# Sums of k's features on halves of TensorE's columns, numerators on their own, projections side by side in a linear-attention and mixture kernel

## The chip, the cores and the metric

The kernel runs on one core of a Trainium2 chip. The metric is the device time of one execution in microseconds (us), lower is better.

## What is computed

The reference, cut to its three stages (B = 8, H = 8 heads, S = 576 positions, D = 64, 128 features):

```python
def phi(x):
    proj = einsum('bhsd,df->bhsf', x, w_phi)
    proj = proj - max(abs(proj), axis=-1, keepdims=True)
    return concatenate([exp(proj), exp(-proj)], axis=-1)
q_p, k_p = phi(q), phi(k)
kv = einsum('bhsf,bhsd->bhfd', k_p, v)          # sums of k's features, with
z = sum(k_p, axis=2)                            # their denominators
num = einsum('bhsf,bhfd->bhsd', q_p, kv)        # numerators
den = einsum('bhsf,bhf->bhs', q_p, z)[..., None] + 1e-06
x = (num / den), heads put side by side         # (8, 576, 512)
# mixture 1: xk, xr from x and x shifted by one; sigmoid(xr @ w_r) * (relu(xk @ w_k)**2 @ w_v)
# mixture 2: sigmoid(causal convolution of 5 taps) * (x @ w_val), then @ w_out
```

## The kernel before

Everything lies in one function, `build`. It doesn't issue instructions in the order of its text. It adds tasks to an `Order` (L99): each names an engine, an assumed duration, what it reads and writes, the new buffers it takes, and a due time. `run` (L129) then walks through time: for every engine it takes, among the tasks sorted by due time, the one that can start first by the assumed durations, and emits its instructions. So each engine has a fixed order, written out ahead; on the chip the instructions wait for one another by semaphores. The due times stand in the table `T` (L33), counted in pairs: `sums=-0.37` means that the sums of pair j are due at j - 0.37.

**The attention stage** works on 32 pairs of heads, j = 0 to 31. Two pairs (n = j // 2) share one load of q, k and v (`load_t` L394, `load_v` L407). For each pair TensorE does these tasks:

- `q_proj`, `k_proj` (L479, L469), both through `proj` and `project` (L418): eight matmuls that contract over 64 rows. The two heads of a pair lie on partitions 0 to 63 and 64 to 127, so one matmul uses the upper half of the array's rows and the next one the lower half. `tails` (L450) does the last 64 positions of q and k for two pairs at once, eight matmuls every second pair. Each takes two PSUM banks of the tag "pj", of which four may be held (`PSB` L241).
- `q_tails`, `q_turn` (L482, L500): ten transposes that turn q's projections.
- `kv` (L520): the sums. Twenty matmuls, each with a stationary block of 128 positions by 128 features (one of exp and exp of the negative) and 65 moving columns of v (64 and a column of ones). The operands are plain f32, and each such matmul is two weight loads and two matmuls in the trace.
- `num` (L562): the numerators, four groups of six matmuls with 288 moving columns and a stationary block of 65 columns, in f32r (one matmul instruction each).

`kv` is called four times a pair, i = 0 to 3, with five sums each, and hands them to `together` (L587), which alternates them with one group of numerators of the pair before: product, sum, product, sum. After the last sums ScalarE and VectorE split the result into a high and a low part (`kvh`, `kvl`), the stationary blocks of the numerators.

The other engines' part: VectorE takes the maximum and subtracts it (`centre` L426), ScalarE does the exponentials and copies, GpSimd subtracts the high parts (`less_far` L271). From pair 2 to 24 the weights of the mixtures are narrowed and split as well (`convert` L339): ScalarE, four operations on VectorE, GpSimd, two transfers a piece, 28 pieces in all. All transfers in this stage are issued by SyncE (SP).

**The mixture stage** (`moe` L678) works on 16 blocks of 288 positions; its matmuls (`gemm` L663, `st_v` L751) have 288 moving columns.

The line that the change is about:

```python
mm(out=b[:, o:o + 65], lhsT=lhs, rhs=vt[:, a:a + 65], start=(k == 0), stop=(c == 3), skip_group_check=True)
```

Of the kernel before, what the change touches and what calls it, by code (L numbers as in the profile page):

```python
# [18 lines left out]
NP = 2 * NQ  # L19
S = 576  # L20
TB = 288
# [4 lines left out]
def pattern(bits):  # L26
# [3 lines left out]
LEAST, MOST = pattern((896 + 128) << 20), pattern(((1150 + 128) << 20) | 0xFFFFF)  # L30


T = dict(load_q=-2.59, load_k=-2.65, load_v=-1.31, tails=-1.05, q_proj=-1.29, k_proj=-1.16, q_tails=-0.19,  # L33
         q_turn=(-0.15, 0.1), sums=-0.37, finish=1.77, convert=0.24)
FROM, TO = 2, 25

LAST = ("pj", "qp", "kv", "cv")
# [3 lines left out]
DMA_START = 1.3  # L41
DMA_END = 1.0
DMA_RATE = 350e3


class Buf:
# [52 lines left out]
class Order:  # L99
# [3 lines left out]
        self.tasks, self.slots, self.queue, self.banks = [], slots, {}, banks  # L103
        self.last_write, self.reads, self.now = {}, {}, 0.0

    def add(self, eng, dur, fn, r=(), w=(), new=(), at=None, dma=0):
        t = {"eng": eng, "dur": dur, "fn": fn, "deps": set(), "at": self.now if at is None else at,
             "id": len(self.tasks), "new": list(new), "dma": dma, "end": None,
             "bufs": set()}
        for x in r:  # L110
            t["deps"].update(self.last_write.get(x, ()))
        for x in w:
            t["deps"].update(self.reads.pop(x, ()))
            t["deps"].update(self.last_write.get(x, ()))
        for x in r:
            self.reads.setdefault(x, []).append(t["id"])
        for x in w:
            self.last_write[x] = [t["id"]]
        for b in new:
            self.queue.setdefault(b.tag, []).append((b, t["id"]))  # L120
        for x in itertools.chain(r, w):
            b = x[0] if isinstance(x, tuple) else x
            if isinstance(b, Buf):
                b.users.append(t["id"])
                t["bufs"].add(b)
        t["deps"].discard(t["id"])
        self.tasks.append(t)

    def run(self):  # L129
        tasks = self.tasks  # L130
        place = {tag: {b: k for k, (b, _) in enumerate(q)} for tag, q in self.queue.items()}
        taken = dict.fromkeys(self.queue, 0)
        free, dma_free = {}, 0.0
        todo = {}
        for t in tasks:
            todo.setdefault(t["eng"], []).append(t)
        for q in todo.values():
            q.sort(key=lambda t: (t["at"], t["id"]))

        def ready(t):  # L140
            at = 0.0
            for d in t["deps"]:
                d = tasks[d]
                if d["end"] is None:
                    return None
                at = max(at, d["end"] + (SAME if d["eng"] == t["eng"] else SEM))
            if any(b.tile is None and b not in t["new"] for b in t["bufs"]):
                return None
            ahead = {}
            banked = [b for b in t["new"] if b.tag in self.banks.most]  # L150
            if banked:
                t["found"] = self.banks.when(tasks, banked)
                if t["found"] is None:
                    return None
                at = max(at, t["found"][-1][0])
            for b in t["new"]:
                k = place[b.tag][b]
                if k != taken[b.tag] + ahead.get(b.tag, 0):
                    return None
                ahead[b.tag] = ahead.get(b.tag, 0) + 1  # L160
                if b.tag in self.banks.most:
                    continue
                old = k - self.slots[b.tag]
                if old >= 0:
                    for u in self.queue[b.tag][old][0].users:
                        u = tasks[u]
                        if u["end"] is None:
                            return None
                        at = max(at, u["end"] + SEM)
            return at  # L170

        left = len(tasks)
        while left:
            best = None
            for eng, q in todo.items():
                f = free.get(eng, 0.0)
                got = None
                for t in q[:400]:
                    at = ready(t)
                    if at is None:  # L180
                        continue
                    at = max(at, f)
                    if got is None or at < got[0] - 1e-9:
                        got = (at, t)
                        if at <= f:
                            break
                if got and (best is None or got[0] < best[0]):
                    best = got
            at, t = best
            banked = [b for b in t["new"] if b.tag in self.banks.most]  # L190
            if banked:
                t["rel"] = {u for _, _, old in t["found"] if old is not None for u in old.users}
                self.banks.take(t["found"], banked)
            for b in t["new"]:
                taken[b.tag] += 1
                if b.tag not in self.banks.most:
                    b.tile = b.make()
            t["fn"]()
            free[t["eng"]] = at + t["dur"]
            t["end"] = at + t["dur"]  # L200
            if t["dma"]:
                dma_free = max(dma_free, at + DMA_START) + t["dma"] / DMA_RATE
                t["end"] = dma_free + DMA_END
            todo[t["eng"]].remove(t)
            if not todo[t["eng"]]:
                del todo[t["eng"]]
            left -= 1
# [27 lines left out]
def build(ctx, tc, qt, kt, vv, wphi, mu, wk, wr, wv, wval, cw, wout, out):  # L235
# [12 lines left out]
    add = G.add  # L248
# [186 lines left out]
    def proj(x, j, tag):  # L435
        n, p = divmod(j, 2)
        bs = [ps("pj"), ps("pj")]
        if tag == "dq":
            t = sb("kl", [128, 2, 4, 128])
            ds = [(lambda ab=ab: t[:, ab], (t, ab), [] if ab else [t]) for ab in range(2)]  # L440
        else:
            ts = [sb(tag, [128, 4, 128]) for _ in range(2)]
            ds = [(lambda t=t: t[:], t, [t]) for t in ts]
        add("PE", 1.08, lambda: project(bs, x[n], [p * 512 + 128 * i for i in range(4)], 0),
            r=cols_of(x[n], n, p) + [("wph", 0), ("wph", 1)], w=bs, new=bs)
        for ab in range(2):
            centre(bs[ab], ds[ab], 4)
        return [d[:2] for d in ds]

    def tails(j):  # L450
# [5 lines left out]
            for i, x in enumerate((qs, ks)):  # L456
                project(bs, x[n], [1024], i)

        add("PE", 0.64, go, r=cols_of(qs[n], n, 2) + cols_of(ks[n], n, 2) + [("wph", 0), ("wph", 1)], w=bs, new=bs)
        for ab in range(2):  # L460
            centre(bs[ab], (lambda ab=ab: d[:, ab], (d, ab), [] if ab else [d]), 2)
        st[j]["dt"] = d
# [57 lines left out]
    def kv(j, i):  # L520
# [12 lines left out]
        def one(k):  # L533
# [5 lines left out]
            else:  # L539
                a = 1040 + 130 * ab + 65 * p  # L540
                lhs = et[:, ab, half, :]
            mm(out=b[:, o:o + 65], lhsT=lhs, rhs=vt[:, a:a + 65], start=(k == 0), stop=(c == 3), skip_group_check=True)  # L542

        mine = list(range(len(todo) * i // 4, len(todo) * (i + 1) // 4))
        need = {ab for c, ab, _ in (todo[k] for k in mine) if c is not None}
        reads = [(s["ek", x], half) for x in need for half in range(2)]
        if any(todo[k][0] is None for k in mine):
            reads += [(et, 0), (et, 1), (vk, "t", 0), (vk, "t", 1)]
        if need:
            reads += [(vk, 0)]  # L550
        here = [] if i else [("pair", j)]
        together(next(st[j - 1 if i else j - 2]["num"]) if j > (0 if i else 1) else None, [lambda k=k: one(k) for k in mine], reads + [(vk, "ones")], [b, *here],
                 [] if i else [b])
        if i < 3:
            return
        h, l = (sb(t, [128, 260], F32R) for t in ("kvh", "kvl"))

# [26 lines left out]

                yield [lambda i=i, one=one: one(i) for i in range(6)], [*a, *e], b, after

    def together(group, sums, r, w, new):  # L587

        if group is None:
            add("PE", 0.217 * len(sums), lambda: [f() for f in sums], r=r, w=w, new=new)  # L590
            return
        prods, reads, b, after = group

        def go():
            for i in range(max(len(prods), len(sums))):
                for f in prods[i:i + 1] + sums[i:i + 1]:
                    f()

        add("PE", t_mm(TB, 6) + 0.165 * len(sums), go, r=r + reads, w=w + [b], new=new + [b])
        after()  # L600

    def finish(j):
# [270 lines left out]
        load(lambda: cwr, lambda: cw.bitcast(I32).rearrange("p (c t) -> p c t", t=2), 20480, w=["cwr"])  # L873
        narrow(lambda: cwr, lambda: cwt, 20, ("cwr", "cwt"))

    def last_num():
        for i, j in enumerate([NP - 2] + [NP - 1] * 4):
            G.now = NP + T["sums"] + i / 8
            together(next(st[j]["num"]), [], [], [], [])

    for j in range(NP):
        n, p = divmod(j, 2)
        st[j] = {}
# [7 lines left out]
        due(j + T["q_tails"], q_tails, j)  # L891
        for ab in range(2):
            due(j + T["q_turn"][ab], q_turn, j, ab)
        for i in range(4):
            due(j + T["sums"] + i / 4, kv, j, i)
        due(j + T["finish"] + 0.5, finish, j)
        if j % 4 == 3:
            due(j + T["finish"] + (1.5 if j < NP - 1 else 0.6), invert, j // 4)
# [2 lines left out]
        if FROM <= j < TO:  # L901
            w = TO - FROM
            for i in range((j - FROM) * len(pieces) // w, (j - FROM + 1) * len(pieces) // w):
                due(j + T["convert"], convert, *pieces[i], j - 1)
    due(NP + T["sums"], last_num)
    for t, _, fn, args in sorted(events, key=lambda e: e[:2]):
        G.now = t
        fn(*args)
# [54 lines left out]
```

## Time and profile before

| | us |
|---|---|
| median of three runs | 1080.18 |
| lowest, highest | 1072.57, 1080.31 |
| profiled execution, its own time | 1071.74 |
| its span, first to last instruction | 1069.8 |

In the profile, TensorE's matmuls are PE and its weight loads PEld; VectorE is DVE, ScalarE ACT, GpSimd POOL, SyncE SP. Matmuls are pipelined: the duration of one reaches into the next, so what a matmul costs is the distance from its start to the next one's start, not its duration. An operand is written as partitions x elements; "128\*65" behind the names is the stationary block's shape, contracted rows by columns.

### The profile page before, as it was taken

What the parts mean: (1) busy time and instruction counts of PE and PEld (TensorE: products, weight loads), DVE (VectorE), ACT (ScalarE), POOL (GpSimd) and SP (SyncE); (2) the same over time, 40 slices, a digit from 0 to 9 for tenths busy, and PEclk for the clock granted to TensorE, in tenths of its full rate; (3) what the DMA queues carried; (4) which work ended last, traced back from release to release, by engine and by line L of the source; (5) the groups of instructions that cost most, each with busy time, mean ns of one, the idle gap of its engine ahead of it and who ended that gap; (6) DMA issues with size and microseconds to landing.
All of it is one profiled execution on the core that took longest, in us unless ns stands there. A gap on an engine that the chain in (4) does not pass through costs nothing.

```text
span 1069.8 us, 22099 instructions
## 1 busy us (share of the span) xinstructions
PE 1060.4 (99%) x8912; PEld 1037.7 (97%) x8912; DVE 739.5 (69%) x1445; ACT 530.6 (50%) x1042; POOL 319.9 (30%) x438
## 2 busy tenths in 40 slices
PE   8999999999999999999999999999999999999998
PEld 8999999999999999999999999999999999999998
DVE  6889898989766486584765847658476584865735
ACT  5888888888878333242332423324233242332423
POOL 3778787888867311101101011010110101100000
PEclk9999999999999999999999999999999999999999
DMA  7567678778835911201112021120211201100001
GB/s 203 143 190 213 186 232 251 233 236 237 251 70 163 311 25 50 62 17 51 45 29 62 15 54 45 29 62 12 56 45 29 61 13 56 45 6 18 13 12 45
DMA packets 88918, 103.71 MB, mean 97 GB/s; under 512 B 44240, under 2 KB 69200, under 8 KB 88432
## 3 DMA queue, kind: packets, MB, share of 16 engines
q1 hardware_dynamic: 88224, 101.64, 32.4%
q8 instruction: 70, 1.15, 0.5%
q10 hardware_dynamic: 592, 0.66, 0.2%
q14 instruction: 32, 0.26, 0.1%
HBM read 72.62 MB, written 29.66 MB: 96 GB/s over the span
## 4 chain that ended last, share of the span: by engine, by line
PE 95%; DMA 3%; DVE 1%; issue 0%; POOL 0%; SPq 0%; ACT 0%; POOLq 0%; ACTq 0%
PE b L673 15%; PE b L672 15%; PE b L671 15%; PE b L542 10%; PE b L577 9%; PE b L423 7%; PE b L764 6%; PE b L762 6%; PE b L763 6%; PE b L507 3%; DMA eh<-wvhl 1%; DMA qf<-xs 1%; DMA el<-wvalhl 1%; PE b L491 1%; PE b L375 0%
## 5 line engine op out<-in xcount | busy, mean ns | idle before, releaser
L282 POOL TENSOR_TENSOR el<-qe,eh 128x288 fp32r<-128x288 f32 x256 | 199.0, 810 | 77.6 <-ACT eh L266 73.2
L717 POOL TENSOR_TENSOR qf<-qf,rb 128x288 f32<-128x288 f32 (+1 forms) x64 | 56.0, 905 | 530.1 <-DMA qf<-xs 445.3
L542 PE MATMUL b<-v,ek 128*128 128x65 f32 x1024 | 158.1, 247 | 0.0
L542 PEld LDWEIGHTS b<-v,ek 128*128 128x128 f32 x1024 | 156.6, 190 | 0.1
L672 PE MATMUL b<-ql,wkh 128*128 128x288 f32 x512 | 151.9, 297 | 0.0
L673 PE MATMUL b<-qh,wkl 128*128 128x288 f32 x512 | 151.8, 296 | 0.0
L671 PE MATMUL b<-qh,wkh 128*128 128x288 f32 x512 | 151.6, 296 | 0.0
L746 ACT ACTIVATE d<-b 128x288 f32<-128x288 f32 x128 | 52.4, 409 | 161.2 <-PE b L673 160.7
L800 DVE SCALAR_TENSOR_TENSOR qh<-kf,cwt,qh 128x288 f32<-128x288 f32 x256 | 124.8, 516 | 2.1
L429 DVE TENSOR_REDUCE m<-b 128x4 f32<-128x512 f32 (+1 forms) x160 | 95.2, 632 | 33.1 <-PE b L423 32.1
L673 PEld LDWEIGHTS b<-qh,wkl 128*128 128x128 f32 x512 | 96.6, 189 | 0.0
L672 PEld LDWEIGHTS b<-ql,wkh 128*128 128x128 f32 x512 | 96.4, 188 | 0.2 <-DVE ql L269 0.2
L671 PEld LDWEIGHTS b<-qh,wkh 128*128 128x128 f32 x512 | 96.3, 188 | 0.0
L511 ACT ACTIVATE qe<-b 128x512 f32<-128x512 f32 x128 | 70.6, 589 | 32.9 <-PE b L507 32.9
L577 PE MATMUL b<-eh,kvh 128*65 128x288 f32 x256 | 86.1, 336 | 0.0
L747 DVE TENSOR_TENSOR d<-d 128x288 f32<-128x288 f32 x64 | 33.4, 522 | 76.1 <-ACT d L746 76.1
L577 PE MATMUL b<-eh,kvl 128*65 128x288 f32 x256 | 83.4, 326 | 0.1
L577 PE MATMUL b<-el,kvh 128*65 128x288 f32 x256 | 83.3, 325 | 0.0
L475 ACT ACTIVATE ek<-d 128x512 f32<-128x512 f32 x128 | 72.9, 620 | 5.7 <-DVE d L431 5.5
L672 PE MATMUL b<-kl,qe 128*128 128x288 f32 x256 | 75.7, 296 | 0.0
L671 PE MATMUL b<-kh,qe 128*128 128x288 f32 x256 | 75.6, 295 | 0.0
L672 PE MATMUL b<-qe,el 128*128 128x288 f32 x256 | 75.4, 295 | 0.0
(146 smaller groups left out, 3056.7 us busy)
## 6 DMA issues: line engine op xcount, KB each, us to landing
xs<-X SPq DMA_DIRECT2D x32, 288.0 KB
kh<-in_kt SPq DMA_DIRECT2D x15, 576.0 KB
qh<-in_qt SPq DMA_DIRECT2D x15, 576.0 KB
v<-in_vv SPq DMA_DIRECT2D x16, 512.0 KB
rb<-rs SPq DMA_DIRECT2D x16, 289.0 KB
qf<-xs SPq DMA_DIRECT2D x8, 578.0 KB
rb<-rs SPq DMA_DIRECT2D x16, 288.0 KB
qf<-xs SPq DMA_DIRECT2D x8, 576.0 KB
```

Of the source, the lines that this page charges most:

```text
L282: nc.gpsimd.tensor_tensor(out=out[:, c], in0=x[:, c], in1=hi[:, c], op=ALU.subtract)
L423: mm(out=bs[ab][:, (at + i) * 128:(at + i + 1) * 128], lhsT=x[r, c:c + 128], rhs=wph[r], start=True, stop=True)
L429: add("DVE", t_dve(128 * n), lambda: nc.vector.tensor_reduce(out=m[:, 0:n, 0], in_=b3[:, 0:n], axis=AX.X, op=ALU.max, apply_absolute_value ...
L475: add("ACT", t_act(512), lambda d=d, e=e, half=half: act(out=e[:, :, half], in_=d(), func=AF.Exp, scale=-1.0 if half else 1.0), r=[tok], w ...
L511: add("ACT", t_act(512), lambda half=half: act(out=e[:, ab, half, 0:512], in_=b[:], func=AF.Exp, scale=-1.0 if half else 1.0), r=[b], w=[( ...
L542: mm(out=b[:, o:o + 65], lhsT=lhs, rhs=vt[:, a:a + 65], start=(k == 0), stop=(c == 3), skip_group_check=True)
L577: mm(out=b[0:65, 0:TB], lhsT=a[x][:, o:o + 65], rhs=e[y][:, half, ts], start=(i == 0), stop=(i == 5))
L671: mm(out=o[:, 0:TB], lhsT=wh, rhs=mov[0][:, c, :], start=(c == 0), stop=False)
L672: mm(out=o[:, 0:TB], lhsT=wh, rhs=mov[1][:, c, :], start=False, stop=False)
L673: mm(out=o[:, 0:TB], lhsT=wl, rhs=mov[0][:, c, :], start=False, stop=(c == kc - 1))
L762: mm(out=o, lhsT=wh, rhs=h(), start=(c == 0), stop=False)
L800: stt(out=g[:, c], in0=a, scalar=cv[:, c, t:t + 1], in1=g[:, c], op0=ALU.mult, op1=ALU.add)
```

## The change

- Every sum is done in two halves of 64 stationary columns: features 0 to 63 go to PSUM partitions 0 to 63, features 64 to 127 to partitions 64 to 127. Each half has the same 65 moving columns. So a sum is four weight loads and four matmuls, with half the columns.
- `together` is gone. The sums come in two tasks a pair, i = 0 (the four tails and the eight sums of the first head) and i = 1 (the eight sums of the second); the numerators are four tasks of six matmuls (`num_step`), due at j + 0.68 and every quarter pair after.
- Tasks carry a mark "split": "rows" for projections, "columns" for sums. When TensorE's last task had a mark, `run` prefers a task with the same mark that can start within 0.6 us and is due within 0.8 pairs of the first in the queue. Entering a split is assumed to take 0.29 us.
- The due times in `T` are others, also those of loads, conversions and stores.

The diff, without the plain change of the constants `SPLIT`, `KV`, `SOON`, `EARLY` to the file's head and without the two lines of `add` that store the mark:

```diff
-T = dict(load_q=-2.59, load_k=-2.65, load_v=-1.31, tails=-1.05, q_proj=-1.29, k_proj=-1.16, q_tails=-0.19,
-         q_turn=(-0.15, 0.1), sums=-0.37, finish=1.77, convert=0.24)
+T = dict(load_q=-2.16, load_k=-2.75, load_v=-1.7, tails=-0.96, q_proj=-1.74, k_proj=-0.93, q_tails=-0.43,
+         q_turn=(-0.11, -0.21), sums=-0.36, num=0.68, finish=1.99, convert=1.07)
...
+SPLIT = 0.29
+KV = 0.125
+SOON, EARLY = 0.6, 0.8
...
+                    if eng == "PE" and split and t["split"] == split and at <= f + SOON and t["at"] <= q[0]["at"] + EARLY:
+                        got = (at, t)
+                        break
                     if got is None or at < got[0] - 1e-9:
                         got = (at, t)
-                        if at <= f:
+                        if at <= f and not (eng == "PE" and split):
                             break
...
+            if t["eng"] == "PE":
+                if t["split"] and t["split"] != split:
+                    t["dur"] += SPLIT
+                split = t["split"]
...
-        add("PE", 1.08, lambda: project(bs, x[n], [p * 512 + 128 * i for i in range(4)], 0),
-            r=cols_of(x[n], n, p) + [("wph", 0), ("wph", 1)], w=bs, new=bs)
+        add("PE", 0.9, lambda: project(bs, x[n], [p * 512 + 128 * i for i in range(4)], 0),
+            r=cols_of(x[n], n, p) + [("wph", 0), ("wph", 1)], w=bs, new=bs, split="rows")
...
-            mm(out=b[:, o:o + 65], lhsT=lhs, rhs=vt[:, a:a + 65], start=(k == 0), stop=(c == 3), skip_group_check=True)
-
-        mine = list(range(len(todo) * i // 4, len(todo) * (i + 1) // 4))
...
+            for y in (slice(0, 64), slice(64, 128)):
+                mm(out=b[y, o:o + 65], lhsT=lhs[:, y], rhs=vt[:, a:a + 65], start=(k == 0), stop=(c == 3),
+                   skip_group_check=True)
+
+        mine = [k for k, (c, ab, _) in enumerate(todo) if (c is None and i == 0) or (c is not None and ab == i)]
...
-        together(next(st[j - 1 if i else j - 2]["num"]) if j > (0 if i else 1) else None, [lambda k=k: one(k) for k in mine], reads + [(vk, "ones")], [b, *here],
-                 [] if i else [b])
-        if i < 3:
+        add("PE", KV * len(mine), lambda: [one(k) for k in mine], r=reads, w=[b, *here], new=[] if i else [b],
+            split="columns")
+        if i < 1:
             return
...
+    def num_step(j):
+        prods, reads, b, after = next(st[j]["num"])
+        add("PE", t_mm(TB, 6), lambda: [f() for f in prods], r=reads, w=[b], new=[b])
         after()
...
+        for i in range(2):
+            due(j + T["sums"] + i / 4, kv, j, i)
         for i in range(4):
-            due(j + T["sums"] + i / 4, kv, j, i)
+            due(j + T["num"] + i / 4, num_step, j)
...
-    due(NP + T["sums"], last_num)
```

## Rows read from the trace of the kernel before

**Rows 1.** The page, part 1: busy time, share of the span, instructions of each engine.

```profile
PE 1060.4 (99%) x8912; PEld 1037.7 (97%) x8912; DVE 739.5 (69%) x1445; ACT 530.6 (50%) x1042; POOL 319.9 (30%) x438
```

**Rows 2.** The page, part 4: the chain that ended last, shares by engine.

```profile
PE 95%; DMA 3%; DVE 1%; issue 0%; POOL 0%; SPq 0%; ACT 0%; POOLq 0%; ACTq 0%
```

**Rows 3.** Windows: length, busy (instructions) of PE, PEld, DVE, ACT, POOL; clock, DMA share, GB/s.

```profile
108.10:245.90 137.80, 137.80 (x1436) 128.75 (x1434) 123.79 (x225) 117.10 (x238) 110.93 (x154) 1.00 0.76 229
288.20:330.50 42.30, 42.30 (x442) 39.53 (x441) 26.67 (x50) 33.55 (x68) 29.00 (x41) 1.00 0.41 96
560.00:760.00 200.00, 200.00 (x1507) 200.00 (x1507) 128.87 (x263) 69.10 (x132) 17.90 (x20) 1.00 0.15 44
```

**Rows 4.** Timeline of PE, projections of k: start us, length us, instructions merged.

```profile
308.27 1.16 PE L423 MATMUL b<-wph,kh 64*128 64x128 f32 x16
...
318.44 1.16 PE L423 MATMUL b<-wph,kh 64*128 64x128 f32 x16
...
329.41 1.16 PE L423 MATMUL b<-wph,kh 64*128 64x128 f32 x16
```

**Rows 5.** Waits from 108.1 to 245.9: us in total, times, longest.

```profile
DVE m L429 <- PE b L423: 6.2, 12, 0.6
DVE X L582 <- PE b L577: 5.0, 8, 0.7
...
ACT qe L511 <- PE b L507: 13.6, 13, 1.2
```

**Rows 6.** Groups of PE by shape, 108.1 to 245.9: busy us, mean ns, idle before.

```profile
L542 PE MATMUL b<-v,ek 128*128 128x65 f32 x416 | 64.6, 246 | 0.0
...
L542 PE MATMUL b<-v,et 128*128 128x65 f32 x104 | 16.2, 247 | 0.0
```

**Rows 7.** Timeline of PE, products and sums in turn.

```profile
304.92 0.33 PE L577 MATMUL b<-el,kvh 128*65 128x288 f32 x1
305.08 0.33 PE L542 MATMUL b<-v,ek 128*128 128x65 f32 x2
...
305.83 0.33 PE L577 MATMUL b<-el,kvh 128*65 128x288 f32 x1
```

**Rows 8.** Timeline of PE, the last 24 products, first and what follows them.

```profile
346.93 0.29 PE L577 MATMUL b<-eh,kvh 128*65 128x288 f32 x1
...
350.10 0.30 PE L671 MATMUL b<-qh,wkh 128*128 128x288 f32 x1
```

**Rows 9.** Timeline of all engines, sums alone at the start.

```profile
20.15 1.06 PE L542 MATMUL b<-v,et 128*128 128x65 f32 x8
...
20.99 1.42 PEld L542 LDWEIGHTS b<-v,ek 128*128 128x128 f32 x12
21.05 1.50 PE L542 MATMUL b<-v,ek 128*128 128x65 f32 x12
```

**Rows 10.** Timeline of PE, projections next to one another at the start.

```profile
7.99 0.39 PE L423 MATMUL b<-wph,qh 64*128 64x128 f32 x4
...
8.44 1.06 PE L423 MATMUL b<-wph,qh 64*128 64x128 f32 x16
```

**Rows 11.** Timeline of PEld, weight loads of products and sums.

```profile
304.89 0.14 PEld L577 LDWEIGHTS b<-el,kvh 128*65 128x65 f32 x1
304.95 0.32 PEld L542 LDWEIGHTS b<-v,ek 128*128 128x128 f32 x2
```

**Rows 12.** Timeline of PE, projections between transposes.

```profile
106.73 0.38 PE L491 MATMUL b<-ident,dq 128*128 128x128 f32 x2
107.04 1.16 PE L423 MATMUL b<-wph,kh 64*128 64x128 f32 x16
108.13 0.66 PE L507 MATMUL b<-ident,kl 128*128 128x128 f32 x4
...
110.36 0.49 PE L423 MATMUL b<-wph,qh 64*128 64x128 f32 x4
...
111.01 0.66 PE L507 MATMUL b<-ident,kl 128*128 128x128 f32 x4
```

More of the change, by code (lines that the diff above doesn't have):

```diff
@@ L104, in __init__, with add @@
         self.last_write, self.reads, self.now = {}, {}, 0.0
-    def add(self, eng, dur, fn, r=(), w=(), new=(), at=None, dma=0):
+    def add(self, eng, dur, fn, r=(), w=(), new=(), at=None, dma=0, split=False):
         t = {"eng": eng, "dur": dur, "fn": fn, "deps": set(), "at": self.now if at is None else at,
-             "id": len(self.tasks), "new": list(new), "dma": dma, "end": None,
+             "id": len(self.tasks), "new": list(new), "dma": dma, "end": None, "split": split,
              "bufs": set()}
@@ L170, in ready @@
             return at
-        left = len(tasks)
+        left, split = len(tasks), False
         while left:
@@ L457, in go @@
                 project(bs, x[n], [1024], i)
-        add("PE", 0.64, go, r=cols_of(qs[n], n, 2) + cols_of(ks[n], n, 2) + [("wph", 0), ("wph", 1)], w=bs, new=bs)
+        add("PE", 0.45, go, r=cols_of(qs[n], n, 2) + cols_of(ks[n], n, 2) + [("wph", 0), ("wph", 1)], w=bs, new=bs, split="rows")
         for ab in range(2):
@@ L541, in one @@
                 lhs = et[:, ab, half, :]
-            mm(out=b[:, o:o + 65], lhsT=lhs, rhs=vt[:, a:a + 65], start=(k == 0), stop=(c == 3), skip_group_check=True)
-        mine = list(range(len(todo) * i // 4, len(todo) * (i + 1) // 4))
-        need = {ab for c, ab, _ in (todo[k] for k in mine) if c is not None}
-        reads = [(s["ek", x], half) for x in need for half in range(2)]
-        if any(todo[k][0] is None for k in mine):
+            for y in (slice(0, 64), slice(64, 128)):
+                mm(out=b[y, o:o + 65], lhsT=lhs[:, y], rhs=vt[:, a:a + 65], start=(k == 0), stop=(c == 3),
+                   skip_group_check=True)
+        mine = [k for k, (c, ab, _) in enumerate(todo) if (c is None and i == 0) or (c is not None and ab == i)]
+        reads = [(s["ek", i], half) for half in range(2)] + [(vk, 0), (vk, "ones")]
+        if i == 0:
             reads += [(et, 0), (et, 1), (vk, "t", 0), (vk, "t", 1)]
-        if need:
-            reads += [(vk, 0)]
         here = [] if i else [("pair", j)]
-        together(next(st[j - 1 if i else j - 2]["num"]) if j > (0 if i else 1) else None, [lambda k=k: one(k) for k in mine], reads + [(vk, "ones")], [b, *here],
-                 [] if i else [b])
-        if i < 3:
+        add("PE", KV * len(mine), lambda: [one(k) for k in mine], r=reads, w=[b, *here], new=[] if i else [b],
+            split="columns")
+        if i < 1:
             return
@@ L585, in num @@
                 yield [lambda i=i, one=one: one(i) for i in range(6)], [*a, *e], b, after
[L587 to L599, printed above, removed]
+    def num_step(j):
+        prods, reads, b, after = next(st[j]["num"])
+        add("PE", t_mm(TB, 6), lambda: [f() for f in prods], r=reads, w=[b], new=[b])
         after()
@@ L874, in small @@
         narrow(lambda: cwr, lambda: cwt, 20, ("cwr", "cwt"))
[L876 to L879, printed above, removed]
     for j in range(NP):
```

## The prediction

> **What bounds the kernel now.** I read the page first. TensorE is busy for 99% of the span [rows 1], and the chain that ended last, followed back, lies on it for 95% of the span [rows 2]. Next the table of windows, because the share is a mean over two stages. In the attention stage with weight conversion (108 to 246 us) TensorE has no idle time, but VectorE is busy 123.79 of 137.80 us and ScalarE 117.10; late in attention (288 to 330 us) VectorE falls to 26.67 of 42.30 us; in the mixture stage (560 to 760 us) TensorE is full again at 200.00 of 200.00 [rows 3]. The granted clock is 1.00 (2.4 GHz) in all of them, so the clock is no term of the sum. The change touches attention alone: I leave the mixture stage, about 345 to 1070 us, as it is.
>
> Attention is a loop over 32 pairs of heads. The timeline of TensorE shows its beat: from one projection of k to the next it is 308.27 to 318.44 us (10.17) and to 329.41 us (10.97); the long one holds the tails [rows 4]. The mean is 10.57 us. The waits of that stage show VectorE and ScalarE waiting for TensorE (6.2, 5.0 and 13.6 us in thirteen pairs) [rows 5]. So the price of TensorE's instructions sets the beat, and VectorE stands close behind it: 123.79 us in thirteen pairs is 9.52 us a pair.
>
> **Sums, before.** A pair has 20 sums, each two weight loads and two matmuls (L542 in the 13 pairs of that window: x416 on ek and x104 on et, so 40 matmuls a pair [rows 6]). They alternate with the numerators' products: three product-and-sum steps take 304.92 to 305.83 us, so 0.303 us a step [rows 7]. Products alone: 24 of them from 346.93 to 350.10 us, 0.132 us each [rows 8]. A sum inside a step therefore costs 0.303 - 0.132 = 0.171 us, and twenty cost 3.42 us. Sums alone go at 0.90 us for 8 matmuls, 0.1125 each, 0.225 a sum [rows 9]. So interleaving gains something today, and the change gives that up.
>
> **Sums, after.** Each sum becomes two halves of 64 columns, one on either half of the array's columns, and the numerators stand by themselves. No row shows columns split. I bound the price from the nearest rows. Below: with the rows split, two instructions run side by side; x8 takes 7.99 to 8.44 us, so 0.1125 us for two matmuls that each move and load 128 columns [rows 10]. Here 65 are moved and 64 loaded, about half: 0.057 a pass, 0.114 a sum of two passes. Above: a load of 65 columns is followed by the next load 0.06 us later (304.89 to 304.95 [rows 11]); if the halves run one after the other, a sum is four such loads, 0.24 us. A gain beyond 0.114 I exclude, since neither loads nor matmuls get shorter than half. I take 0.12, two passes of one 0.06 load, because the split of rows in this very trace shows both halves side by side, and the split of columns is nearest to it. Twenty sums: 2.40 us.
>
> **The price of a split.** One projection of x16 runs 107.04 to 108.13 us, 1.09 us, though 16 matmuls at the side-by-side rate are 0.90; the two transposes before it begin at 106.73 and should take 0.22, but it starts 0.31 later [rows 12]. So entering and leaving costs 0.19 + 0.09 = 0.28 us. The tails, x8 in 110.36 to 111.01 us, are 0.65 instead of 0.45 by the same [rows 12]. For the split of columns I take 0.28 too; below, nothing (gain 0.28 a pair), above, two entries a pair if a pair's two groups stand apart (loss 0.28). I take one, since the second group is due a quarter of a pair behind the first and the order now prefers a task of the same split.
>
> So the sums gain 3.42 - 2.40 - 0.28 = 0.74 us a pair.
>
> **Projections together.** Before, a pair enters the split of rows 2.5 times (q, k, and the tails every second pair, each apart in [rows 4, 12]). After, their due times within a pair are 0.04 (tails), 0.07 (k) and 0.26 (q), close enough to stand together. At startup the trace has such a row of projections: between 7.99 and 8.44 us no entry is paid [rows 10]. But the projections' four PSUM banks hold only two of the three, and VectorE must free one. I take 1.5 entries a pair, a gain of 0.28; the bounds are nothing and 0.42. Whatever TensorE waits to keep them together (the order allows 0.6 us) comes off this.
>
> **What costs nothing, and its cover.** Numerators now follow their own sums by a whole pair, as far as before; kvh and kvl have that pair as cover. Loads of q, k, v, the converted pieces and the stores are only due at other times: the DMA queues are busy 0.76 of the conversion stage [rows 3], so the same bytes in 10% less time are 0.84. Without that cover a late load of q or k (one array of 128 x 1152 words, 0.59 MB) at the stage's 229 GB/s costs 2.6 us every second pair, more than the gain; I see no queue near that. Past SP no more transfers are issued than before.
>
> **The sum.** TensorE needs 0.74 + 0.28 = 1.02 us less, 9.55 us a pair. VectorE needs 9.52 [rows 3], so in conversion (23 pairs, 2 to 24) two engines would be full at once, in fixed orders that wait for each other. I give half of the gain there, 0.51 us: 23 x 0.51 = 11.7. In the other 9 pairs VectorE is at 63% (26.67 of 42.30) and all of it stays: 9 x 1.02 = 9.2. Together 20.9 us. The profiled execution took 1071.74 us (span 1069.8), so 1051 us. The runs' median, 1080.18, lies 0.8% above it, and the fastest, 1072.57, beside it; I stay with the profiled one and let the range reach up.
>
> **Rivals.**
>
> *The halves don't overlap.* Each half's load and matmul take their turn: at 0.24 us a sum (four loads of 0.06; two passes of a 0.06 load and a 0.057 matmul in turn come to 0.234, the same), twenty cost 4.80, the sums lose 1.66 and the projections return 0.28: 1.38 a pair, 44 us in all, 1116 us. The entry (0.28) and the gain of the projections (0.28) cancel, so it turns where twenty sums cost 3.42, at 0.171 us a sum. At 0.20 it is 32 x 0.58 = 19 us, 1090 us. For it: the trace shows only rows split, and 160 short instructions a pair must be issued. Against it: with rows split, eight loads and eight matmuls run in 0.45 us [rows 10]. The Trainium skill's page "TensorE: Matmul & The Clock Gate", Part 3, "The mechanism", says that weight loads overlap running matmuls only when their row groups differ; by that rule two column halves, which share all rows, would load and multiply in turn, and the time would be this rival's. The trace doesn't bear it out for whole-array sums: twelve loads from 20.99 us and twelve matmuls from 21.05 us lie over each other [rows 9]. Chance 0.15.
>
> *VectorE takes over the bound.* In conversion the beat falls only to 10.4 us, because VectorE's own 9.52 us meets PSUM banks that it frees late. 23 x 0.15 + 9 x 0.6 = 9 us, 1063 us, within 1%. For it: the 90% share. Against it: its idle time today ends on TensorE [rows 5], so it has room to follow. Chance 0.21.
>
> *TensorE gains all.* VectorE hides, the tails stand with k and q: 32 x 1.02 = 33 us, 1039 us; a sum at 0.114 (0.12 a pair) and the projections' 0.42 (0.14 more) would add 32 x 0.26 = 8. Chance 0.14.
>
> *The forecast*, a beat of 9.9 to 10.2 in conversion and 9.5 to 9.7 after, 1044 to 1060 us. Chance 0.50.
>
> **How the numbers follow.** About 1% (11 us) is what a measurement of this kernel tells from no change. Faster by more: the forecast (0.50) and all of the gain (0.14), 0.64. Within: VectorE's bound and a mild loss on the halves, 0.22. Slower by more: the rest of the halves' case, 0.14. The range leaves out the two ends: below 1036 those two together, above 1076 most of the first rival. Cases of both signs don't hold most of the chance, but the forecast's own range is 1044 to 1060.
>
> **What would show it.** In the changed profile: 80 matmuls a pair on the sums' line, with loads of 64 columns, whose starts come every 0.03 us on average (right) or 0.06 (rival); one gap of some 0.2 us around them; k, q and tails in one row of projections; a beat near 10.0 in conversion and 9.55 after it, with first idle time of TensorE ahead of projections, ended by VectorE; and a mixture stage of unchanged length. Wrong would be sums longer than 3.4 us a pair, or a beat still at 10.5 with TensorE idle.

## The result, and the profile after

| | kernel before | changed kernel |
|---|---|---|
| median of the runs, us | 1080.08 | 1034.10 |
| lowest, highest | 1072.57, 1080.31 | 1033.65, 1035.54 |
| profiled execution, its own time | 1071.74 | 1034.55 |
| its span | 1069.8 | 1032.7 |

The ratio of the times is 0.959, with an interval of 0.955 to 0.964: 4.1% faster. Beside the runs of the experiments below the kernel before took 1071.35 and 1071.12 us in the median, and the changed kernel 1033.94 and 1035.11: ratios of 0.965 and 0.966, so about 3.5%, the better figure because it rests on more runs. Of those eighteen later runs of the kernel before, the seven with a mean granted clock of 1.000 took 1068.99 to 1070.96 us, the nine at 0.998 took 1070.87 to 1072.22, and the two at 0.992 took 1078.46 and 1078.51. The sign was right; the size was larger than forecast, and 1034.1 us lies just below the range (1036 to 1076). Between the two profiled executions 37.2 us went, where I had worked out 20.9.

The page of the changed kernel, busy time and instructions. Beside [rows 1], TensorE has 1280 more matmuls and weight loads, and is busy for 37 us less:

```profile
PE 1023.4 (99%) x10192; PEld 998.9 (97%) x10192; DVE 731.0 (71%) x1445; ACT 525.5 (51%) x1042; POOL 320.6 (31%) x438
```

The windows of the changed kernel, in the columns of [rows 3]: the middle of conversion, late attention, and 200 us of the mixture stage.

```profile
105.00:230.00 125.00, 124.44 (x1974) 114.85 (x1970) 121.78 (x225) 116.00 (x240) 113.35 (x158) 1.00 0.86 257
...
270.00:310.00 40.00, 39.33 (x602) 36.72 (x601) 28.52 (x51) 36.19 (x74) 31.87 (x42) 1.00 0.54 146
...
520.00:720.00 200.00, 200.00 (x1511) 200.00 (x1510) 130.52 (x267) 69.50 (x133) 17.89 (x20) 1.00 0.15 43
```

The mixture stage runs as before, 1511 matmuls in 200 us against 1507. In conversion VectorE now works for 121.78 of 125 us, and TensorE for 124.44.

The timeline of TensorE in the changed kernel, start and length in us. It answers to [rows 4, 7 and 12]:

```profile
153.31 1.09 PE L519 MATMUL b<-ident,kl 128*128 128x128 f32 x8
...
191.84 1.09 PE L519 MATMUL b<-ident,kl 128*128 128x128 f32 x8
...
197.21 1.16 PE L435 MATMUL b<-wph,qh 64*128 64x128 f32 x16
198.21 1.06 PE L435 MATMUL b<-wph,kh 64*128 64x128 f32 x16
199.20 0.34 PE L588 MATMUL b<-eh,kvh 128*65 128x288 f32 x1
...
200.03 0.38 PE L503 MATMUL b<-ident,dq 128*128 128x128 f32 x2
200.34 0.69 PE L555 MATMUL b<-v,et 128*64 128x65 f32 x16
200.86 2.04 PE L555 MATMUL b<-v,ek 128*64 128x65 f32 x64
202.83 1.09 PE L519 MATMUL b<-ident,kl 128*128 128x128 f32 x8
203.85 1.16 PE L435 MATMUL b<-wph,qh 64*128 64x128 f32 x16
204.94 0.35 PE L588 MATMUL b<-eh,kvh 128*65 128x288 f32 x1
...
208.17 0.38 PE L503 MATMUL b<-ident,dq 128*128 128x128 f32 x2
```

Four pairs now take 153.31 to 191.84 us, 9.63 us a pair; before it was 10.57. A sum is now four matmuls in the trace, two for each half, so a pair has eighty half matmuls. All of them stand in one stretch: 16 need 0.52 us (200.34 to 200.86, the entry of about 0.05 inside), the next 64 need 1.97 with the exit. At 0.117 us a sum (that is 0.0292 for each half matmul, worked out from 64 of them in 1.87 us without the exit of about 0.1) twenty are 2.34; the stretch takes 2.49, and it begins 0.31 us after two transposes that need 0.22. q's and k's projections stand together at 197.21 and 198.21, and q's stands alone at 203.85. The 24 products from 204.94 to 208.17 are 3.23 us.

### The profile page after: what moved, and what is told of

It is laid out like the page before. It is cut to its first block, busy times and chain, and to the rows that moved or that the text cites. A ratio compares the mean times of both kernels' runs of the same rounds, so it can differ in the third digit from the quotient of the medians.

```text
span 1032.7 us, 24612 instructions
## 1 busy us (share of the span) xinstructions
PE 1023.4 (99%) x10192; PEld 998.9 (97%) x10192; DVE 731.0 (71%) x1445; ACT 525.5 (51%) x1042; POOL 320.6 (31%) x438
## 4 chain that ended last, share of the span: by engine, by line
PE 89%; ACT 3%; POOL 3%; DMA 2%; DVE 2%; issue 1%; SPq 0%; POOLq 0%; ACTq 0%
PE b L674 16%; PE b L673 16%; PE b L672 16%; PE b L588 8%; PE b L763 6%; PE b L764 6%; PE b L765 6%; PE b L435 6%; PE b L555 6%; PE b L519 3%; POOL el L294 2%; ACT ek L487 1%; ACT eh L278 1%; DMA qf<-xs 1%; DMA xs<-X 1%
## 5 line engine op out<-in xcount | busy, mean ns | idle before, releaser
L588 PE MATMUL b<-eh,kvh 128*65 128x288 f32 x256 | 77.9, 304 | 0.0
L673 PE MATMUL b<-qe,el 128*128 128x288 f32 x256 | 75.5, 295 | 0.0
L588 PE MATMUL b<-el,kvh 128*65 128x288 f32 x256 | 75.3, 294 | 0.2 <-POOL el L294 0.2
L588 PE MATMUL b<-eh,kvl 128*65 128x288 f32 x256 | 75.2, 294 | 0.0
L672 PE MATMUL b<-qe,el 128*128 128x288 f32 x256 | 75.1, 293 | 0.0
L278 ACT ACTIVATE eh<-qe 128x1152 fp32r<-128x1152 f32 x64 | 74.8, 1168 | 0.0
L673 PE MATMUL b<-eh,X 128*128 128x288 f32 x240 | 70.7, 295 | 0.0
```

The source lines that it names most:

```text
L278: act(out=out, in_=x, func=AF.Copy)
L588: mm(out=b[0:65, 0:TB], lhsT=a[x][:, o:o + 65], rhs=e[y][:, half, ts], start=(i == 0), stop=(i == 5))
L672: mm(out=o[:, 0:TB], lhsT=wh, rhs=mov[0][:, c, :], start=(c == 0), stop=False)
L673: mm(out=o[:, 0:TB], lhsT=wh, rhs=mov[1][:, c, :], start=False, stop=False)
```

## Experiments

Three theories stood against one another after the result. A: TensorE's own instructions set the beat, at 0.117 us a sum and about 0.28 for each entry into a split, and nothing else holds it. B: the order is what gained (numerators apart, projections together, due times), or, in conversion, VectorE takes part of the gain. C: what looks like a price of the split is something else, such as the issue of short instructions. The kernel before ran beside each of three groups. The runs with sums on the full array, with lower halves first and with halves in the old order are one execution each, beside one of the kernel before; the others are medians, beside the changed kernel once more at 1033.94 us (kernel before 1071.35) or 1035.11 us (1071.12).

> The changed kernel once more, as the measure for the three beside it on the same chip: 1033.6 to 1035.6 us, 0.96 of the kernel before.

> The changed kernel once more, as the measure for the three beside it on the same chip: 1033.5 to 1035.5 us.

**Sums on the full array again, in the changed order.**

```diff
-            for y in (slice(0, 64), slice(64, 128)):
-                mm(out=b[y, o:o + 65], lhsT=lhs[:, y], rhs=vt[:, a:a + 65], start=(k == 0), stop=(c == 3),
-                   skip_group_check=True)
+            mm(out=b[:, o:o + 65], lhsT=lhs, rhs=vt[:, a:a + 65], start=(k == 0), stop=(c == 3), skip_group_check=True)
```

> The changed kernel, same order on every engine, but each sum is again one matmul over all 128 columns. Theory A (the halves side by side are the gain): in the kernel before, sums alone cost 0.225 us each [rows 9], in the changed one two halves cost 0.117; 20 x 0.108 = 2.16 us a pair dearer, less about 0.25 for the entry that falls away: 32 x 1.9 = 61 us, 1034 + 61 = about 1095 us, slower than the kernel before. Rival B (the gain is in the order: numerators apart, projections together, other due times): 1035 to 1050 us.

Measured: 1087.38 us, beside 1070.02 for the kernel before. The timeline of TensorE:

```profile
198.43 1.00 PE L554 MATMUL b<-v,et 128*128 128x65 f32 x8
199.27 3.74 PE L554 MATMUL b<-v,ek 128*128 128x65 f32 x32
202.84 1.04 PE L519 MATMUL b<-ident,kl 128*128 128x128 f32 x8
```

The 40 matmuls of a pair take 198.43 to 202.84, 4.41 us, where the 80 halves took 2.49. So theory A holds and B, that the order alone gains, falls: without the halves the new order is 17 us slower than the old one. A sum costs 0.22 us here (4.41 / 20), where it cost 0.171 between products: that the lost cover is the whole reason is argued from these two prices. The time lies 8 us under theory A's number; 0.22 in place of 0.225 a sum is about 3 of them, and the rest is not settled.

**All lower halves first, then all upper ones.**

```diff
-        add("PE", KV * len(mine), lambda: [one(k) for k in mine], r=reads, w=[b, *here], new=[] if i else [b],
+        add("PE", KV * len(mine), lambda: [one(k, y) for y in (slice(0, 64), slice(64, 128)) for k in mine], r=reads, w=[b, *here], new=[] if i else [b],
```

> The changed kernel, but within each task of sums all lower halves come first and then all upper halves. Theory A (two halves overlap only where neighbours in the queue lie on different column halves): each half costs a load or matmul of its own, about 0.058 us where it now shares it, so 0.234 us a sum, 2.34 us a pair, 1034 + 75 = about 1109 us. Rival B (a short load and a short matmul are simply issued at 0.03 us each, whatever half they lie on): 1034 us.

Measured: 1086.49 us. The timeline of TensorE, at a change from lower to upper halves (et is first in each half's row, ek follows) and at the end of a pair's sums:

```profile
210.70 0.92 PE L554 MATMUL b<-v,ek 128*64 128x65 f32 x13
211.41 0.27 PE L554 MATMUL b<-v,et 128*64 128x65 f32 x1
211.46 0.22 PE L554 MATMUL b<-v,ek 128*64 128x65 f32 x1
211.51 0.22 PE L554 MATMUL b<-v,et 128*64 128x65 f32 x1
211.52 0.22 PE L554 MATMUL b<-v,ek 128*64 128x65 f32 x1
211.57 0.22 PE L554 MATMUL b<-v,et 128*64 128x65 f32 x1
211.57 0.22 PE L554 MATMUL b<-v,ek 128*64 128x65 f32 x1
...
213.67 0.86 PE L554 MATMUL b<-v,ek 128*64 128x65 f32 x12
```

Twelve halves on the same columns last 0.86 us, the last one 0.22 of it, so they start every 0.058 us: (0.86 - 0.22) / 11. That is the price theory A gives, 0.234 us a sum, and it rules out theory C, that short instructions are simply cheap to issue. Two things follow. The halves gain only when neighbours in the order lie on different column halves. And 0.058 us is about what one load of 65 columns alone took in the kernel before (0.06 [rows 11]), so load and matmul don't take turns: on the same rows and columns the next load overlaps the running matmul. The total was 23 us under the expectation. Where the order changes from one half to the other, about three matmuls of the second half start among the last of the first, up to 0.16 us early (211.41 against 211.57); I had not thought of that. A pair has three such changes, so that is some 15 of the 23 us; the rest is not settled.

**The halves alone, in the old order.** The kernel before, with the two half matmuls in place of one.

```diff
-            mm(out=b[:, o:o + 65], lhsT=lhs, rhs=vt[:, a:a + 65], start=(k == 0), stop=(c == 3), skip_group_check=True)
+            for y in (slice(0, 64), slice(64, 128)):
+                mm(out=b[y, o:o + 65], lhsT=lhs[:, y], rhs=vt[:, a:a + 65], start=(k == 0), stop=(c == 3),
+                   skip_group_check=True)
```

> The kernel before with the halves alone: sums and numerators still alternate, order as before. Theory A (each change between split and whole array costs about 0.25 us in and out): a step of product and sum costs 0.132 + 0.117 + 0.25 = 0.50 us where it cost 0.303, 20 x 0.20 = 3.9 us a pair, 1072 + 126 = about 1198 us. Rival B (the change costs only between long stretches, a lone sum between products hides it): 0.249 us a step, about 1037 us.

Measured: 1213.60 us, 144 more than the kernel before beside it. The timeline of TensorE, one step of product and sum and the next product:

```profile
299.73 0.34 PE L579 MATMUL b<-el,kvh 128*65 128x288 f32 x1
300.00 0.34 PE L543 MATMUL b<-v,ek 128*64 128x65 f32 x4
300.27 0.34 PE L579 MATMUL b<-eh,kvl 128*65 128x288 f32 x1
```

A step takes 0.54 us, where it took 0.303 [rows 7]; theory A had 0.50. Less 0.132 for the product and 0.117 for the sum, in and out of the split is 0.29 us, close to the 0.28 that the split of rows showed [rows 12]. This is the reason why the numerators had to leave the sums: with halves in turn the gain of 0.05 us a sum costs 0.29.

**Projections apart.** In the changed kernel the preference holds for sums alone, and q and k are due elsewhere.

```diff
-                    if eng == "PE" and split and t["split"] == split and at <= f + SOON and t["at"] <= q[0]["at"] + EARLY:
+                    if eng == "PE" and split and split == "columns" and t["split"] == split and at <= f + SOON and t["at"] <= q[0]["at"] + EARLY:
...
-T = dict(load_q=-2.16, load_k=-2.75, load_v=-1.7, tails=-0.96, q_proj=-1.74, k_proj=-0.93, q_tails=-0.43,
+T = dict(load_q=-2.16, load_k=-2.75, load_v=-1.7, tails=-0.96, q_proj=-1.24, k_proj=-0.73, q_tails=-0.43,
```

> The changed kernel with the projections apart: the preference for the same split holds for sums alone, and q and k are due at other quarters of a pair, so TensorE's order has 77 stretches of projections instead of 46. Theory A (TensorE alone sets the beat, each entry into a split costs 0.28 us): 31 x 0.28 = 8.7 us, 1034 + 8.7 = 1043 us. Rival B (in conversion VectorE is the bound and swallows what TensorE spends): only the pairs outside conversion pay, 9 of 32: 2.4 us, 1036 to 1037 us.

Measured: 1053.06 us, 19 more than the changed kernel beside it. Neither number holds. The entries themselves are there (77 stretches), but in this order TensorE also waits, as its waits from 105 to 230 us show; the changed kernel is idle for 0.56 us in all there:

```profile
PE b L435 <- ACT X L278: 2.8, 2, 1.7
PE b L555 <- ACT ek L487: 1.5, 3, 0.6
PE b L588 <- ACT qe L523: 0.9, 2, 0.5
```

So this run mixes two things. Up to its last matmul TensorE is idle for 14.1 us, against 4.6 in the changed kernel beside it: 9.5 us, which with 8.7 for the entries are 18 of the 19. I asked again with the due times left alone.

**No preference for projections, same due times.** Only the first of the two edits above.

> The changed kernel with its own due times, but the preference for the same split holds for sums alone: TensorE's order has 63 stretches of projections instead of 46 (33 stretches of sums become 32). It asks again what the kernel with the projections apart left open, where waits came on top of the entries. Theory A (an entry costs 0.28 us and nothing else changes): 17 x 0.28 = 4.8 us, 1039 us. Rival B (leaving the neighbours apart makes TensorE wait as well, as it did there): 10 us or more, over 1043 us.

Measured: 1043.15 us, 8.0 more than the changed kernel. It lies between the two theories: 4.8 us are the 17 entries by count. In the trace TensorE's idle stretches over 0.1 us from 270 us on, where attention gives way to the mixtures, add up to 3.0 us, against 1.0 in the changed kernel. The remaining microsecond is not settled; the four runs spread from 1041.54 to 1045.04 us.

**Projections together, and nothing else.** The kernel before, with the mark, the preference and the assumed 0.9, 0.45 and 0.29 us for projections; sums and due times untouched.

> The kernel before with one part of the change alone: projections carry the mark and stand together, sums stay on the whole array in turn with numerators, due times as before. TensorE's order has 48 stretches of projections instead of 76. Theory A (0.28 us for each entry, TensorE sets the beat): 28 x 0.28 = 7.8 us less than the kernel before, ratio 0.993. Rival B (projections that stand together make others late, since the two PSUM banks that the third needs are freed by VectorE): no gain, ratio 0.998 to 1.01.

Measured: 1064.86 us, ratio 0.9930 with an interval of 0.9903 to 0.9958. Theory A's 0.993 is met: 28 entries fewer by 0.28 us.

**One operation more on VectorE for each piece of weights.**

```diff
         add("DVE", t_dve(n), s1, w=[y])
+        add("DVE", t_dve(n), s1, w=[y])
```

> The changed kernel with one more operation on VectorE for each of the 28 pieces of weights (the clamp twice), 0.69 us each, 19 us in all. In the changed kernel VectorE is busy 121.78 of 125 us in the middle of conversion, TensorE 124.44. Theory A (VectorE is near its bound and fills its gap first): 230 us of conversion hold about 6 us of gap, so 13 us more, 1047 us. Rival B (VectorE is already a bound together with TensorE): all of it, 1053 us. Rival C (its busy share overstates how full it is): under 5 us, 1034 to 1039 us.

Measured: 1044.41 us, 10.5 more than the changed kernel beside it. The window of the middle of conversion:

```profile
105.00:230.00 125.00, 121.43 (x1907) 111.24 (x1907) 124.83 (x232) 111.97 (x231) 106.72 (x148) 1.00 0.80 243
```

VectorE is now full (124.83 of 125), and TensorE has idle time. Of 19 us of added work at least 9 didn't show in the time. The 10.5 that did aren't VectorE's alone, because the order is worked out anew with the added tasks: it has 40 stretches of sums for 33 and 47 of projections for 46, eight entries or some 2 us. In this window the bound has changed hands, with VectorE busy for 2.5% more time than in the changed kernel.

**Two operations fewer on VectorE.** The clamp and the shift of each piece are left out, so this kernel's weights, and its output, are not the reference's; the rest of the work is the same.

```diff
-        add("DVE", t_dve(n), s1, w=[y])
-        add("DVE", t_dve(n), s2, w=[y])
```

> The changed kernel without two of the four operations that narrow a piece of weights (the clamp and the shift are left out, so the weights are not the right ones): 28 x 2 x 0.69 = 39 us less on VectorE. Theory A (TensorE alone sets the beat): at most its idle time in conversion comes back, 0.56 of 125 us, so 1033 to 1034 us. Rival B (the step of my prediction: two full engines in fixed orders cost each other time): 3 us or more, under 1031 us.

Measured: 1033.89 us, the changed kernel beside it 1033.94. The same window:

```profile
105.00:230.00 125.00, 125.00 (x2002) 115.51 (x1998) 102.22 (x194) 116.76 (x244) 114.33 (x159) 1.00 0.85 261
```

VectorE's work in the window falls from 121.76 to 102.22 us and the time doesn't move. This run is the verdict on the step of my prediction that halved the gain. It isn't quite nothing that VectorE took, though: TensorE does 2002 matmuls in the window where it did 1974. The timeline shows the same, at the first sums of pairs 4 and 24, the changed kernel first, then this run:

```profile
47.14 0.69 PE L555 MATMUL b<-v,et 128*64 128x65 f32 x16
...
238.61 0.69 PE L555 MATMUL b<-v,et 128*64 128x65 f32 x16
```

```profile
47.02 0.69 PE L553 MATMUL b<-v,et 128*64 128x65 f32 x16
...
235.70 0.69 PE L553 MATMUL b<-v,et 128*64 128x65 f32 x16
```

Twenty pairs take 188.68 us in place of 191.47, 9.43 a pair in place of 9.57. So VectorE's work, or the order that was worked out around it, cost 0.14 us a pair; I had withheld 0.51. Behind pair 24 this run loses its lead again, and why isn't settled: TensorE's idle stretches over 0.1 us from 270 us on add up to 1.7 us, against 1.0 in the changed kernel.

**Other due times.** The changed kernel with `load_k=-3.07, load_v=-1.58, tails=-0.93, q_proj=-1.58, k_proj=-0.92, q_tails=-0.57, q_turn=(-0.11, 0.02), num=0.71, finish=2.06, convert=1.22`, `SPLIT = 0.27`, `KV = 0.12` and 0.4 us for the wait that the preference allows.

> The changed kernel with other due times and assumed durations nearer to what the trace shows (0.12 us for a sum, 0.27 for an entry); the work is the same, 47 stretches of projections, 32 of sums. Theory A (what is left in attention is TensorE's own work; it idles about 9 us in the whole span, 2.4 of them before its first matmul): at most 3 to 5 us less, 1029 to 1031 us. Rival B (VectorE, at 97% in conversion, holds it): the same time within 2 us.

Measured: 1027.79 us, ratio 0.9591 to the kernel before (0.9569 to 0.9613), and 7.3 us under the changed kernel beside it. The window:

```profile
105.00:230.00 125.00, 125.00 (x2002) 115.63 (x2000) 122.50 (x228) 118.39 (x243) 113.75 (x158) 1.00 0.86 253
```

TensorE has no idle time left there, with the same instructions and nearly as many entries (47 and 32). It is faster than either kernel, by more than I had put down for what was left. The beat from pair 4 to 24 is 9.43 us (46.84 to 235.50), the same as with two operations fewer on VectorE, but with all of VectorE's work: so the 0.14 us a pair can be had by the order alone. Of the 5.6 us between the profiled spans (1032.0 and 1026.4) these pairs are 2.8, and 1.5 lie behind the start of the last matmul.

## Why the prediction was right or wrong

**What bounds the kernel: right.** TensorE set the beat before and sets it after; the mixture stage is unchanged, as the windows show.

**The price of a half: right.** 0.12 us a sum was taken, 0.117 came. The rival in which the halves load and multiply in turn is refuted: the changed timeline shows 64 half matmuls in 1.97 us. The rule of the Trainium skill that I had set beside that rival ("TensorE: Matmul & The Clock Gate", Part 3, "The mechanism": weight loads overlap running matmuls only across row groups) isn't borne out by the run with all lower halves first either, where halves on the same rows and columns start every 0.058 us, and not every 0.117 us, as a load (0.06) and a matmul (0.057) in turn would.

**The price of an entry: right.** 0.28 us was taken for columns by analogy with rows; the run with halves in the old order gives 0.29. In the changed kernel the stretch itself gives 0.15 (2.49 less 2.34) and 0.09 ahead of it, 0.24, without what the transposes behind it lose. One entry a pair is what came (33 stretches of sums for 32 pairs).

**The sums' gain: near, by errors that cancel.** I had 0.74 us a pair. The old stretches of sums and products take, in the pair of 10.17 us from 308.27 us on, 309.77 to 311.50, 311.86 to 313.68 and 314.77 to 318.13 us: 1.73 + 1.82 + 3.36 = 6.91 us. I had put them together from 20 steps of 0.303 and four products of 0.132, 6.59, and left out what the beginnings of the groups and the products next to each other cost. The new ones are 2.49 + 3.23 and 0.09 ahead of the split, 5.81. By these stretches the gain was 1.10 us a pair. But the old ones also hold the late starts of the projections behind them, and behind the new split transposes start late, which I had left out: eight take 1.02 us (202.83 to 203.85), at 0.11 they are 0.88. The balance of whole pairs holds everything, from each matmul's start to the next one's, pairs 4 to 24: sums and products 6.96 us before and 5.87 after, transposes 1.11 and 1.33, projections 2.51 and 2.37, together 10.57 and 9.57. Sums, products and transposes together gained 0.86. The lines of the old kernel's timeline on which the first account stands:

```profile
309.77 0.38 PE L577 MATMUL b<-eh,kvh 128*65 128x288 f32 x1
...
311.50 0.60 PE L507 MATMUL b<-ident,kl 128*128 128x128 f32 x4
311.86 0.37 PE L577 MATMUL b<-eh,kvh 128*65 128x288 f32 x1
...
313.68 1.16 PE L423 MATMUL b<-wph,qh 64*128 64x128 f32 x16
314.77 0.35 PE L577 MATMUL b<-eh,kvh 128*65 128x288 f32 x1
...
318.13 0.38 PE L491 MATMUL b<-ident,dq 128*128 128x128 f32 x2
```

**Projections together: right.** 46 stretches came for 76, that is 30 x 0.28 = 8.4 us by count, 0.26 us a pair against 0.28 forecast; the kernel with this part alone gained 0.7%. In the balance above 0.14 of it stand with the projections themselves; 0.09 of an entry is a late start [rows 12], which the balance puts on the instruction ahead.

**TensorE's beat: right.** 9.55 us was the sum; 9.57 came from pair 4 to 24, and 9.63 in the four pairs above. The gain of 1.00 us a pair meets the 1.02 of the sum, though its parts were partly mis-sized.

**VectorE takes half of the gain in conversion: wrong.** This is the step that failed. I argued that two engines that both need 9.5 us a pair in fixed orders must wait for each other, and gave up 11.7 us, 0.51 a pair. The changed kernel kept 1.00 of the 1.02 us a pair there, with TensorE busy 124.44 and VectorE 121.78 of 125 us. The run with 39 us less on VectorE didn't move the time and its beat fell by 0.14 us a pair, which other due times give as well; the run with 19 us more took only 10.5 us longer. What I had read as a warning, VectorE's 90% with its idle time ended by TensorE [rows 5], was the sign of an engine that follows. Its waits from 105 to 230 us in the changed kernel, in the first line, are down to one kind, and TensorE isn't named in it. One of my signs didn't come either: I had expected TensorE to be idle ahead of projections, until VectorE was done. What it waits for there, in the second line, are the exponentials of k from ScalarE, ahead of sums:

```profile
DVE b L325 <- ACT b L322: 2.4, 3, 0.9
...
PE b L555 <- ACT ek L487: 0.5, 3, 0.2
```

So the rival in which VectorE takes over the bound fell, and the one in which TensorE gains all, to which I had given 0.14, is what happened: its 1039 us, less about 5 more at both ends of attention. At its start the first transposes of q's projections come at 10.70 us instead of 13.15, and from the last projection to the last matmul there are 733.9 us instead of 736.2.

**What hangs together.** 23 pairs by the 0.51 us that I withheld are 11.7 us; the two ends are 2.4 + 2.3. Together 16.4, and the forecast was off by 16.3 (37.2 - 20.9). That it closes so well is luck in part: from the first transposes to the last projection 33.8 us went, where 32 pairs by 1.02 are 32.6, and from the end of the last matmul to the end of the span the changed kernel takes 1.4 us more. Nor was the clock no term, as I had read from three windows behind 108 us: at the start of the kernel before it was lower, as the last section shows.

## What to carry to other kernels

In this kernel, with 128 stationary columns against 65 moving ones, two halves on different column halves run side by side and nearly halve the price of a sum (0.225 to 0.117 us), but only as neighbours in the order and in long stretches: each way in and out of a split costs about 0.28 us, more than one whole sum. An engine at 90% whose idle time mostly ends on the bounding engine need not be a second bound; before giving up part of a gain to it, ask what it would wait for, or take some of its work away and see, in the beat of that stage and not in the total alone. And when two streams are priced from the distance of their steps, take whole pairs, beginnings and junctions and neighbours too, for the old kernel as well as for the new one.

## What the runs showed of the hardware that was not expected

Matmuls of one column half can start before earlier ones of the other half: in the run with all lower halves first, a matmul of the upper half starts at 211.41 us, ahead of three of the lower half at 211.46, 211.52 and 211.57 that stand before it in the order.

TensorE's granted clock in the beginning differs. In the kernel before, TensorE had waited twice for 0.94 us, at 10.4 and 12.5 us, and the granted clock in the window behind was 0.61 on the mean, part of it at 1.2 GHz: eight transposes that need 0.11 us each at 2.4 GHz start every 0.21 us. In the changed kernel TensorE waits 0.18 us at that place and the clock stays at 1.00 (2.4 GHz); it had waited once for 0.88 us, up to 7.75 us, and the windows behind that, to 13 us, show 1.00 too. First the kernel before (window, then timeline), then the changed one:

```profile
13.10:17.00 3.90, 3.90 (x25) 3.83 (x26) 3.90 (x8) 3.72 (x10) 0.00 (x0) 0.61 1.05 323
```

```profile
12.54 0.81 PE L491 MATMUL b<-ident,dq 128*128 128x128 f32 x2 [0.94 <-DVE dq L431]
13.15 1.91 PE L507 MATMUL b<-ident,kl 128*128 128x128 f32 x8
14.85 0.53 PE L542 MATMUL b<-v,et 128*128 128x65 f32 x2
```

```profile
13.00:17.00 4.00, 4.00 (x106) 3.81 (x104) 4.00 (x8) 4.00 (x9) 1.18 (x2) 1.00 0.85 257
```

```profile
10.21 0.66 PE L503 MATMUL b<-ident,dq 128*128 128x128 f32 x2 [0.18 <-DVE dq L443]
10.70 1.04 PE L519 MATMUL b<-ident,kl 128*128 128x128 f32 x8
```

That the clock is the reason for the 2.4 us at the beginning was not tested by a run of its own; eight transposes at half the clock are 0.8 us of it. Among the later runs of the kernel before, listed with the result, those at 1.000 lie 1.4 us below those at 0.998 in the median.
